# Attention and MLP in one kernel: the opening's loads, row copies, memsets and transposes in another order

## The chip, the cores and the metric

The kernel runs on one core of one Trainium2 chip. The metric is the device time of one execution in microseconds (us); the profile shows one such execution, taken by the hardware profiler. The engines are named as in the profile: PE is TensorE (matrix products, PEld its weight loads), DVE is VectorE, ACT is ScalarE, POOL is GpSimd, SP is SyncE, which here only issues transfers. SBUF is the memory on the core from which the engines work, PSUM the banks into which TensorE writes. "L311" is line 311 of the kernel.

## What is computed

Eight batches of causal attention with eight heads of 64 columns over 576 positions, with a decay that is a running sum of log f, and after it a two-layer MLP with a nonlinearity:

```python
scale = 1.0 / np.sqrt(D)
scores = scale * np.matmul(q, k.transpose(0, 1, 3, 2))
cum = np.cumsum(np.log(np.clip(f, 0.0001, 1.0)), axis=-1)
decay = cum[:, :, :, None] - cum[:, :, None, :]
scores = np.where(causal, -1000000000.0, scores + decay)
attn = np.exp(scores - np.max(scores, axis=-1, keepdims=True))
attn = attn / (np.sum(attn, axis=-1, keepdims=True) + 1e-09)
x = np.matmul(attn, v)            # then heads side by side: 4608 x 512
h = x @ w_in                      # w_in 512 x 2048
out = (h - np.tanh(h)) @ w_out    # w_out 2048 x 512
```

## The kernel before

**Pairs and tiles.** The work goes by pairs of heads: four pairs a batch, 32 in all. A pair has seven score tiles, numbered ti 0 to 6; tiles 0 to 2 belong to its first head, 4 to 6 to its second, tile 3 (`LAST`) holds the small last blocks of both. A score tile is some matrix products into a PSUM bank (L352; in batch 0 the causal mask is added by a further product with `late`, L355), an exp on ScalarE (L361, output `e`, or `el` for tile 3) and, from batch 1 on, a masking select on GpSimd (L371). `values` (L389) multiplies the exps with v; `divide` (L398 to L400) scales the result on VectorE into `xn`; `turn` brings xn into `XR`, the MLP's input, in batch 0 by a TensorE transpose and a copy (L417 to L421).

**Transposed q and k.** `trans` turns a pair's q or k on TensorE (six small products, L298) into a PSUM bank and copies it in two halves to QT or KT; the string handed over says by which engine and when: "V" VectorE (L311), "A" ScalarE (L309); a pair of letters listed in the line `now = ...` (before: "VA" and "Vv") has its second half put off until `rest` is called. With "AV" both halves are issued at once. Before pair 0, `split` gives four copies of 288 columns in place of two of 576.

**Decay rows.** QT and KT have 67 rows: 64 of the head, and three that bring the decay into the product. They are made from the running sum `cum` (scan, L187) as two fp16 parts, `chi` (L189) and `clo` (L190). For head 0 of batch 0 the rows are written by engines: QT's by ScalarE (L572), KT's by the VectorE copy of L191. The other heads' rows are transfers from chi and clo, made by `bulk` for batch 0 (two on SP's queue, one on GpSimd's, L211 to L213) and by `load_aug` for the later batches.

**Loads.** Nearly all loads are issued by GpSimd, in program order with its other work: q and k by pairs of heads (`load_qk`, L102), v by a whole head (`load_v_head`, L127), by a block of positions (`load_v_block`, L131), and the last 64 positions of all heads (`load_v_rest`, L123); w_in in two parts (L222), w_out in two (L226). Those of the body stand in the table `LOADS`, keyed by (pair, tile).

**Order.** It is written out by hand: `start` (L570) has the transposes of pair 0, its first two score tiles, and filler products on `warm` (`unread`, L566, results unused); then `bulk`, and then for each pair the list that `att_items` makes, tile by tile, with MLP pieces between its items from pair 4 on. `mlp1` (L451, tanh at L456, sum at L462) works a 128-column tile of w_in at a time, `mlp2_plain` (L492) and `mlp2` (L517) the second layer. Each engine takes its instructions in program order and waits where one's inputs or banks aren't ready. The exps have ten buffers, score tiles two banks (a third in batch 0), the early transposes three.

**Memsets.** Batch 0's padding is cleared by VectorE near the top; batch 1's (KT's padding columns, the unused rows of v's last block, v's column of ones, the third `el` buffer) by GpSimd in `last`, issued in pair 1.

Of the kernel before, what the change touches and what calls it, by code (L numbers as in the profile page):

```python
# [9 lines left out]
FP16 = mybir.dt.float16  # L10
# [4 lines left out]
PITCH = 640  # L15
VW = 66
# [5 lines left out]
def kernel(  # L22
# [10 lines left out]
    nc = tc.nc  # L33
# [96 lines left out]
    def load_v_block(b, n, h0, h1):  # L130
# [13 lines left out]
    nc.scalar.activation(out=expo, in_=warm[0:1, 0:1], func=AF.Ln)  # L144
    id16 = cst.tile([P, P], FP16)
    nc.vector.memset(id16, 0.0)
    nc.gpsimd.affine_select(out=id16, in_=id16, compare_op=ALU.not_equal,
                            fill=1.0, base=0, pattern=[[-1, P]], channel_multiplier=1)
    load_qk(qn, q, 0, 0, 2)
# [12 lines left out]
    per = cst.tile([NX, 6], FP32)  # L162
    nc.vector.memset(vn[0][D:P, NJ - 1, :, :], 0.0)
    mul_k, add_k, mul_l, mul_q, add_q, both = (per[:, i:i + 1] for i in range(6))
    EL = [cst.tile([P, 192], FP16, tag=f"el{i}", name=f"el{i}") for i in range(3)]
    load_v_rest(0)
    load_v_head(0, 0)
    load_v_head(0, 1)
    nc.gpsimd.affine_select(out=late, in_=late, compare_op=ALU.is_ge, fill=-60000.0,
                            base=0, pattern=[[1, P]], channel_multiplier=-1)  # L170

    r_hi, r_one = (id16[0:NX, NH + g:NH + g + 1] for g in (0, 2))
    nc.vector.tensor_scalar(out=both, in0=r_one, scalar1=-inv_qscale, scalar2=inv_qscale, op0=ALU.mult, op1=ALU.add)
# [5 lines left out]
    for e in EL[0:2]:  # L179
        nc.vector.memset(e, 0.0)  # L180
    nc.vector.tensor_scalar(out=lf, in0=lf, scalar1=0.0001, scalar2=1.0,
                            op0=ALU.max, op1=ALU.min)
    nc.vector.memset(vn[0][:, :, :, D:VW], 1.0)
    nc.scalar.activation(out=lf, in_=lf, func=AF.Ln)
    nc.scalar.activation(out=expo, in_=lf[0:1, 0:1], func=AF.Exp)
    cum = TQ[0][0:NX, :, :].rearrange("p c s -> p (c s)").bitcast(FP32)[:, S:2 * S]
# [1 line left out]
                                 op0=ALU.mult, op1=ALU.add)  # L188
    nc.vector.tensor_scalar(out=chi, in0=cum, scalar1=mul_k, scalar2=add_k, op0=ALU.mult, op1=ALU.add)  # L189
    nc.vector.scalar_tensor_tensor(out=clo, in0=cum, scalar=mul_l, in1=chi, op0=ALU.mult, op1=ALU.subtract)  # L190
    nc.vector.tensor_copy(out=KT[0][NH:NX, 0, 0:S], in_=clo[NH:NX, :])  # L191

    def aug_rows(b):
        i, h0 = b % 2, 0 if b else 1
# [12 lines left out]
    const_rows(0)  # L207

    def bulk():
        (k_hi, chi_0), (k_lo, clo_0), (q_hi, _) = aug_rows(0)  # L210
        nc.sync.dma_start(out=k_hi, in_=chi_0)  # L211
        nc.gpsimd.dma_start(out=q_hi, in_=chi_0)
        nc.sync.dma_start(out=k_lo, in_=clo_0)  # L213
        load_qk(qn, q, 0, 4, 6)
        load_qk(kn, k, 0, 4, 6)
        load_qk(qn, q, 0, 6, H)
        load_qk(kn, k, 0, 6, H)
        for n in range(NJ - 1):
            load_v_block(0, n, 2, H)
# [5 lines left out]
    def load_wout(e0, e1):  # L225
        nc.gpsimd.dma_start(out=wout[:, :, e0:e1], in_=moe_w_out[:, e0:e1].rearrange("(t p) e -> p t e", p=P))  # L226

    LOADS = {(0, 1): [lambda: load_qk(qn, q, 1, 0, 2), lambda: load_qk(kn, k, 1, 0, 2)],
             (0, 4): [lambda: load_qk(qn, q, 1, 2, 4), lambda: load_qk(kn, k, 1, 2, 4)],
             (1, 0): [lambda: load_win(0, DFF // 2)],  # L230
             (1, 2): [lambda: load_qk(qn, q, 1, 4, H)],
             (1, 5): [lambda: load_qk(kn, k, 1, 4, H)],
             (2, 1): [lambda: load_v_rest(1), lambda: load_v_head(1, 0)],
             (2, 4): [lambda: load_v_head(1, 1), lambda: load_win(DFF // 2, DFF)],
             (4, 0): [lambda: load_wout(0, HE)],
             (5, 1): [lambda: load_wout(HE, DM)]}
    for n in range(NJ - 1):
# [49 lines left out]
    def trans(b, c, src, dst, early, copies, split=False):  # L287
        pn, g3 = S // NT6, NT6 // 2
        if early:
            t32 = m_bank("t32")  # L290
        elif KEPT and src is kn:
            t32 = ps_m.tile([P, UW], FP32, tag=f"m{KEPT[0]}", name="t32")
        else:
            t32 = ps_tr.tile([P, UW], FP32, tag="tr", name="t32")
        t16 = t32.bitcast(FP16)[:, 0:2 * S // 2].rearrange("p (a g n) -> p a g n", a=2, g=g3)
        for a in range(2):
            for g in range(g3):
                nc.tensor.transpose(out=t16[:, a, g, :],  # L298
                                    in_=src[b % 2][:, 2 * c + a, 2 * g:2 * g + 2, :],
                                    identity=id16[0:pn, 0:pn])  # L300
        parts = [(a, e) for a in range(2) for e in range(2)] if split else [(slice(0, 2), e) for e in range(2)]

        def copy(a, e, eng):
            if split:
                a = slice(a, a + 1)
            to = dst[b % 2][0:D, 2 * c:2 * c + 2, e:S:2].rearrange("d a (p g) -> d a p g", g=g3)[:, a]
            of = t16[e * D:(e + 1) * D, :, :, :].rearrange("d a g p -> d a p g")[:, a]
            if eng == "A":
                nc.scalar.activation(out=to, in_=of, func=AF.Copy)  # L309
            else:  # L310
                nc.vector.tensor_copy(out=to, in_=of)  # L311

        todo = [lambda a=a, e=e, eng=eng: copy(a, e, eng) for (a, e), eng in zip(parts, copies)]
        now = 1 if copies in ("VA", "Vv") else 2
        for fn in todo[:now]:
            fn()
        if now == 1:
            LATER.extend(todo[now:])
        return todo[now:]
# [250 lines left out]
    def start():  # L570
        unread(47)
        nc.scalar.activation(out=QT[0][NH:NX, 0, :], in_=cum[NH:NX, :], func=AF.Identity, bias=add_q[NH:NX, :], scale=mul_q[NH:NX, :])  # L572
        q_rest = trans(*pairs[0], qn, QT, True, "AAAA", True)
        for fn in q_rest:
            fn()
        unread(6)
        k_rest = trans(*pairs[0], kn, KT, True, "VVVV", True)
        unread(34)
        scores(*pairs[0], 0)
        for fn in k_rest:  # L580
            fn()
        scores(*pairs[0], 1)
        unread(2)

    def last():
        nc.gpsimd.memset(KT[1][:, :, S:PITCH], 0.0)
        nc.gpsimd.memset(vn[1][D:P, NJ - 1, :, :], 0.0)
        nc.gpsimd.memset(vn[1][:, :, :, D:VW], 1.0)
        nc.gpsimd.memset(EL[2], 0.0)

    def att_items(p):
        def put(fn, *args):
# [7 lines left out]
        for ti in range(len(TILES)):  # L600
# [4 lines left out]
                items.append((lambda: load_aug(1), False))  # L605
            if p == 0 and ti in (2, 5, 6):
                put(unread, {2: 6, 5: 4, 6: 2}[ti])
            if p == 1 and ti == 3:
                put(last)
            for load in LOADS.get((p, ti), ()):  # L610
                items.append((load, False))
            at_q, at_k = (1, 2) if p == 0 else (None, 0) if early else (0, 2) if p == NPAIR else (0, 3)
            if ti == 5 and p < NPAIR - 1:
                put(trans, *pairs[p + 2], qn, QT, True, "VV")
            if p in (2 * NPAIR - 1, 2 * NPAIR, 2 * NPAIR + 1) and (ti % 2 or ti == 0):
                items.append((rest, False))
# [7 lines left out]
                    put(mlp1, 0, ti - 4, 1)  # L624
                    items.append((rest, False))
            if ti == at_k and p < 2 * NPAIR - 1 and p != NPAIR:
                put(trans, *after, kn, KT, early, "AV" if p in (0, 2) else "VV")
            if p == NPAIR:
                if ti == 0:
                    put(turn, *pairs[1])  # L630
                elif ti == 1:
                    put(turn, *pairs[p - 2])
                    put(values, *before)
                    put(mlp1, 0, 0, 0)
                elif ti == 2:
                    put(mlp1, 0, 1, 0)
                    put(turn, *before, True)
                    put(trans, *after, kn, KT, early, "Vv")
            elif early and ti in (2, 4) and before:
                put(values, *before, (ti // 2 - 1,))  # L640
            elif not early and ti == 2 and before:
                put(values, *before, (0, 1), p == NPAIR + 2)
            if p < NPAIR:
# [70 lines left out]
```

## Time and profile before

| | us |
|---|---|
| median of 3 runs | 338.89 (338.81 to 339.19) |
| profiled execution | 338.77 |
| its span, first to last instruction | 337.1 |
| first scores of pair 0 (L352) | 9.12 |
| first exp (L361) | 9.60 |
| first product of mlp1 (L451) | 27.28 |
| first part of w_in landed | 26.2 |
| second part of w_in landed | 35.3 |

The landings are an issue's start plus the time to landing that the profile gives for it (16.05 + 10.1 and 21.89 + 13.4). The landings of the other loads that matter here, in the same way: q and k of heads 0, 1 at 5.05 and 5.8; of heads 2, 3 at 7.65 and 8.4; the rest of v at 8.8, value heads 0 and 1 at 9.4 and 10.3; the chi rows of QT at 10.9; q and k of heads 4, 5 at 11.1 and 12.0; of heads 6, 7 at 14.2 and 14.7; the four value blocks at 15.6, 16.4, 17.0 and 17.6.

How to read it: a timeline row gives the start, the duration, the engine, the line, the operation with its output and inputs and shapes, how many follow each other, and in brackets the time that the engine stood idle before it and what ended this. Pieces of the chain of waits follow each other in time; each was released by the one before it. PE counts as busy also with filler products.

### The profile page before, as it was taken

The page shows a single profiled execution, that of the slowest core. Times are in us where ns is not written, and L with a number is a line of the kernel's source. Part 1 is how long each engine was busy: PE and PEld are TensorE (multiplying, and loading weights), DVE is VectorE, ACT ScalarE, POOL GpSimd, SP SyncE. Part 2 cuts the span into 40 slices and gives each one's busy share as a digit, 9 for nine tenths or more (in the row PEclk, how much of TensorE's full clock was granted, in tenths as well). Part 3 has the DMA queues.
Part 4 walks back from the last instruction along what each step waited for, and adds up shares of the span by engine and source line. Part 5 has one row for each costly group of instructions (what it writes and reads, how often), then busy time and mean ns, then how long its engine had stood idle before and what let it go on. Part 6 is the DMA issues. An engine that isn't in the chain of part 4 may idle for free.

```text
span 337.1 us, 8726 instructions
## 1 busy us (share of the span) xinstructions
PE 330.0 (98%) x3313; PEld 235.6 (70%) x3313; DVE 260.8 (77%) x509; ACT 233.2 (69%) x438; POOL 163.2 (48%) x321
## 2 busy tenths in 40 slices
PE   8899999999999999999999999999999999999996
PEld 8775558875687558845888888656865686486485
DVE  7998986659887886778867896788668866966865
ACT  6997777978977886788677867787558733632630
POOL 8977467775667564767377637722322210000000
PEclk9999999999999999999999999999999999999999
DMA  9999999999979997999899999990130022002003
GB/s 113 143 203 202 186 198 165 184 159 172 142 87 190 136 134 72 164 152 139 94 122 187 118 112 117 163 132 18 51 113 2 19 65 97 2 31 95 0 12 116
DMA packets 147468, 38.82 MB, mean 115 GB/s; under 512 B 128181, under 2 KB 146335, under 8 KB 147426
## 3 DMA queue, kind: packets, MB, share of 16 engines
q0 software_dynamic: 94528, 18.37, 75.5%
q1 hardware_dynamic: 52892, 19.89, 32.4%
q8 instruction: 26, 0.43, 0.6%
q14 instruction: 16, 0.13, 0.2%
q10 hardware_dynamic: 6, 0.01, 0.0%
HBM read 36.85 MB, written 9.44 MB: 137 GB/s over the span
## 4 chain that ended last, share of the span: by engine, by line
PE 90%; DVE 7%; ACT 2%; issue 1%; ACTq 0%
PE hps L451 36%; PE ops L517 29%; PE ps L352 11%; PE av L389 8%; PE ops L492 4%; DVE KT L311 2%; DVE QT L311 1%; PE t L298 1%; ACT e L361 1%; DVE xn L400 1%; DVE gq L462 0%; DVE TQ L187 0%; ACT th L456 0%; PE x L417 0%; DVE clo L190 0%
## 5 line engine op out<-in xcount | busy, mean ns | idle before, releaser
L451 PE MATMUL hps<-XR,win 128*128 128x512 f16 (+1 forms) x640 | 140.7, 357 | 0.3 <-DVE gq L462 0.3
L456 ACT ACTIVATE th<-hps 128x512 f32<-128x512 f32 x144 | 86.6, 602 | 55.5 <-PE hps L451 53.5
L361 ACT ACTIVATE e<-ps 128x512 f16<-128x512 f32 x192 | 110.2, 597 | 8.9 <-PE ps L352 7.4
L462 DVE TENSOR_TENSOR gq<-hps,th 128x512 f16<-128x512 f32 x144 | 98.0, 687 | 23.6 <-ACT th L456 22.0
L371 POOL TENSOR_SCALAR_AFFINE_SELECT e<-e 128x128 f16<-128x128 f16 x168 | 60.7, 364 | 71.5 <-ACT e L361 68.7
L451 PEld LDWEIGHTS <-win 128*128 128x128 f16 x640 | 57.7, 97 | 49.0 <-issue 1.1
L352 PE MATMUL ps<-QT,KT 67*128 67x64 f16 (+4 forms) x384 | 76.5, 276 | 2.0 <-DVE KT L311 1.4
L517 PEld LDWEIGHTS <-gq 128*128 128x128 f16 x640 | 60.3, 97 | 11.1
L517 PE MATMUL ops<-wout,gq 128*128 128x256 f16 x512 | 63.2, 272 | 0.0
L352 PEld LDWEIGHTS <-KT 67*128 67x128 f16 x384 | 36.4, 98 | 23.4 <-DVE KT L311 2.0
L389 PEld LDWEIGHTS <-e 128*128 128x128 f16 x896 | 32.3, 97 | 3.6
L389 PE MATMUL av<-vn,e 128*128 128x65 f16 x896 | 33.6, 193 | 0.0
L517 PE MATMUL ops<-W,sq 128*128 128x256 f16 x256 | 31.2, 272 | 0.0
L131 POOL DMA_DIRECT2D vn<-in_v_dram x32 | 28.0, 877 | 6.5 <-DMA win<-in_moe_w_in_dram 2.9
L400 DVE TENSOR_TENSOR xn<-av,rs 128x640 f16<-128x640 f32 x32 | 26.4, 825 | 1.3 <-DVE rs L399 0.2
L517 PEld LDWEIGHTS <-sq 128*128 128x128 f16 x256 | 24.1, 97 | 3.4
L108 POOL DMA_DIRECT2D kn<-in_k_dram x25 | 21.2, 848 | 2.1 <-issue 1.8
L108 POOL DMA_DIRECT2D qn<-in_q_dram x25 | 21.2, 848 | 1.8 <-issue 1.4
L371 POOL TENSOR_SCALAR_AFFINE_SELECT el<-el 128x128 f16<-128x128 f16 x28 | 9.3, 333 | 26.1 <-ACT el L361 25.8
L398 DVE TENSOR_SCALAR rs<-av 128x10 f32<-128x10 f32 x32 | 5.2, 163 | 18.2 <-PE av L389 17.0
L532 ACT ACTIVATE m<-ops 128x512 f32<-128x512 f32 x16 | 9.5, 596 | 10.9 <-PE ops L517 10.9
L484 DVE TENSOR_TENSOR gq<-gq 128x512 f16<-128x512 f16 x32 | 17.1, 533 | 0.0
(83 smaller groups left out, 311.8 us busy)
## 6 DMA issues: line engine op xcount, KB each, us to landing
out_dram<-ost SPq DMA_DIRECT2D x34, 256.0 KB
vn<-in_v_dram POOLq DMA_DIRECT2D x24, 128.0 KB, 6.2
qn<-in_q_dram POOLq DMA_DIRECT2D x20, 128.0 KB, 5.0
kn<-in_k_dram POOLq DMA_DIRECT2D x20, 128.0 KB, 5.6
win<-in_moe_w_in_dram POOLq DMA_DIRECT2D x2, 1024.0 KB, 11.8
wout<-in_moe_w_out_dram POOLq DMA_DIRECT2D x2, 1024.0 KB, 15.6
XR<-xn SPq DMA_TRANSPOSE x56
qn<-in_q_dram POOLq DMA_DIRECT2D x6, 144.0 KB, 4.6
```

The costliest lines, as they stand in the source:

```text
L108: nc.gpsimd.dma_start(out=dst[b % 2][0:pn, n, :].rearrange("p (h d) -> p h d", h=H), in_=src[b, :, n * P:n * P + pn, :].rearrange("h p d - ...
L131: nc.gpsimd.dma_start(out=vn[b % 2][:, n, h0:h1, 0:D], in_=v[b, h0:h1, n * P:(n + 1) * P, :].rearrange("h p d -> p h d"))
L352: nc.tensor.matmul(out=ps[:, col:col + n], lhsT=kt[0:rows, h, j * P:(j + 1) * P], rhs=qt[0:rows, h, i0:i0 + n], start=True, stop=cut == 0)
L361: nc.scalar.activation(out=e[:, lo:hi], in_=ps[:, lo:hi], func=AF.Exp, bias=-SHIFT, scale=qscale)
L371: nc.gpsimd.affine_select(out=view, in_=view, compare_op=ALU.is_ge, fill=0.0, base=0, pattern=pat, channel_multiplier=-1)
L389: nc.tensor.matmul(out=av[:, a, ib, :], lhsT=E.pop((b, c, a, j, ib)), rhs=vn[b % 2][:, j, 2 * c + a, 0:D + 1], start=(j == 0), stop=(j == ib))
L400: nc.vector.tensor_tensor(out=xn.rearrange("p i (a d) -> p a i d", a=2), in0=av[:, :, :, 0:D], in1=rs.to_broadcast([P, 2, NJ, D]), op=ALU. ...
L451: nc.tensor.matmul(out=hps[:, o:o + n], lhsT=win[:, ci, ft * P:(ft + 1) * P], rhs=XR[:, ci, t:t + n], start=(ci == 0), stop=(ci == NCH - 1))
L456: nc.scalar.activation(out=th, in_=hps, func=AF.Tanh, scale=-1.0)
L462: nc.vector.tensor_tensor(out=GQ[(u, i)][:, half, kt, :], in0=hps, in1=th, op=ALU.add)
L484: nc.vector.tensor_tensor(out=LHS[name](u, i)[:, ks], in0=LHS[x](u, i)[:, ks], in1=LHS[y](u, i)[:, ks], op=op)
L517: nc.tensor.matmul(out=ps[:, m, :], lhsT=LHS[lhs](u, kt // 4)[:, kt % 4, m * P:(m + 1) * P], rhs=rhs[:, kt, :], start=(fresh and (apart or ...
```

## The change

In words, in program order:

- The third `el` buffer's memset and KT[1]'s padding move up: the padding to GpSimd's front, ahead of the select that makes the identity; the `el` memset behind the select that makes `late`.
- Q's heads 4, 5 of batch 0 are loaded right behind the first four loads; value head 0 then goes ahead of the rest of v; value head 1 moves into `bulk`, behind k's heads 4, 5.
- The two memsets of vn[1] move to VectorE, behind the clip of f.
- The transfer of the chi rows to QT moves out of `bulk`, ahead of the copy of clo's rows into KT, and that copy is made by GpSimd instead of VectorE.
- w_in is split 7:9 tiles instead of 8:8; its first part is issued in (0, 4), where k's heads 2, 3 of batch 1 stood, and these move to (1, 0).
- Pair 1's k copies go by "Av" (ScalarE's half at once, VectorE's put off) instead of "AV". Pair 2's q is transposed at tile 3 of pair 0 (by "Vv", with `rest` right behind) instead of tile 5. Pairs 3 and 4 have q transposed at tile 6 instead of 5.
- Pair 1's first values come at tile 3 of pair 2 instead of tile 2.
- Three filler products fewer (31 for 34) ahead of the first scores.

```diff
+    EL = [cst.tile([P, 192], FP16, tag=f"el{i}", name=f"el{i}") for i in range(3)]
+    nc.gpsimd.memset(KT[1][:, :, S:PITCH], 0.0)
     nc.gpsimd.affine_select(out=id16, in_=id16, compare_op=ALU.not_equal,
...
-    EL = [cst.tile([P, 192], FP16, tag=f"el{i}", name=f"el{i}") for i in range(3)]
+    load_qk(qn, q, 0, 4, 6)
+    load_v_head(0, 0)
     load_v_rest(0)
-    load_v_head(0, 0)
-    load_v_head(0, 1)
     nc.gpsimd.affine_select(out=late, in_=late, compare_op=ALU.is_ge, fill=-60000.0,
                             base=0, pattern=[[1, P]], channel_multiplier=-1)
+    nc.gpsimd.memset(EL[2], 0.0)
...
-    nc.vector.memset(vn[0][:, :, :, D:VW], 1.0)
+    nc.vector.memset(vn[1][D:P, NJ - 1, :, :], 0.0)
+    for t in vn:
+        nc.vector.memset(t[:, :, :, D:VW], 1.0)
...
-    nc.vector.tensor_copy(out=KT[0][NH:NX, 0, 0:S], in_=clo[NH:NX, :])
+    nc.gpsimd.dma_start(out=QT[0][D + 2:D + 3, 1:H, :], in_=chi[1:H, :])
+    nc.gpsimd.tensor_copy(out=KT[0][NH:NX, 0, 0:S], in_=clo[NH:NX, :])
...
     def bulk():
-        (k_hi, chi_0), (k_lo, clo_0), (q_hi, _) = aug_rows(0)
+        (k_hi, chi_0), (k_lo, clo_0), _ = aug_rows(0)
         nc.sync.dma_start(out=k_hi, in_=chi_0)
-        nc.gpsimd.dma_start(out=q_hi, in_=chi_0)
         nc.sync.dma_start(out=k_lo, in_=clo_0)
-        load_qk(qn, q, 0, 4, 6)
         load_qk(kn, k, 0, 4, 6)
+        load_v_head(0, 1)
         load_qk(qn, q, 0, 6, H)
...
+    WF = 7 * P
...
-             (0, 4): [lambda: load_qk(qn, q, 1, 2, 4), lambda: load_qk(kn, k, 1, 2, 4)],
-             (1, 0): [lambda: load_win(0, DFF // 2)],
+             (0, 4): [lambda: load_qk(qn, q, 1, 2, 4), lambda: load_win(0, WF)],
+             (1, 0): [lambda: load_qk(kn, k, 1, 2, 4)],
...
-             (2, 4): [lambda: load_v_head(1, 1), lambda: load_win(DFF // 2, DFF)],
+             (2, 4): [lambda: load_v_head(1, 1), lambda: load_win(WF, DFF)],
...
-        now = 1 if copies in ("VA", "Vv") else 2
+        now = 1 if copies in ("VA", "Vv", "Av") else 2
...
-        unread(34)
+        unread(31)
...
-    def last():
-        nc.gpsimd.memset(KT[1][:, :, S:PITCH], 0.0)
-        nc.gpsimd.memset(vn[1][D:P, NJ - 1, :, :], 0.0)
-        nc.gpsimd.memset(vn[1][:, :, :, D:VW], 1.0)
-        nc.gpsimd.memset(EL[2], 0.0)
...
-            if p == 1 and ti == 3:
-                put(last)
...
-            if ti == 5 and p < NPAIR - 1:
+            if ti == 6 and 0 < p < NPAIR - 1:
                 put(trans, *pairs[p + 2], qn, QT, True, "VV")
...
-                put(trans, *after, kn, KT, early, "AV" if p in (0, 2) else "VV")
+                put(trans, *after, kn, KT, early, "Av" if p == 0 else "AV" if p == 2 else "VV")
+            if p == 0 and ti == 3:
+                put(trans, *pairs[2], qn, QT, True, "Vv")
+                items.append((rest, False))
...
-            elif early and ti in (2, 4) and before:
-                put(values, *before, (ti // 2 - 1,))
+            elif early and ti in (3 if p == 2 else 2, 4) and before:
+                put(values, *before, (ti // 4,))
```

## The prediction

> **What bounds the kernel now.** I read the page first, then the chain of waits of the first 45 us, then the timelines of ScalarE, VectorE, GpSimd and TensorE up to 40 us, then the landing of each load. The page says where a saving can count at all:
>
> ```profile
> PE 330.0 (98%) x3313; PEld 235.6 (70%) x3313; DVE 260.8 (77%) x509; ACT 233.2 (69%) x438; POOL 163.2 (48%) x321
> ```
>
> TensorE is busy for 330.0 of 337.1 us, and its work in the body isn't touched. Between 36 and 60 us it is busy 23.77 of 24. So the change can only move the time at which this full stretch begins; whatever it saves in the opening arrives at the end once, undiluted. What sets that time is in the chain of waits of the opening (start, duration, piece):
>
> ```profile
> 6.91 0.83 DVE clo L190
> 7.74 0.02 issue
> 7.76 0.30 DVE KT L191
> 8.06 0.03 issue
> 8.09 0.47 DVE KT L311
> 8.57 0.01 issue
> 8.58 0.49 DVE KT L311
> 9.07 0.05 issue
> 9.12 0.39 PE ps L352
> ...
> 11.38 0.81 ACT KT L309
> 12.19 0.02 issue
> 12.22 0.81 DVE KT L311
> ...
> 25.21 0.84 DVE xn L400
> 26.05 0.04 issue
> 26.09 0.45 PE x L417 x5
> ```
>
> The reader is to see VectorE in nearly every piece: clo, the 0.30 us copy of its rows into KT, the two copies for head 0, the first scores at 9.12; after a detour over ScalarE, VectorE again from 12.22 to 26.05, where TensorE takes over. But ScalarE is nearly as full (its timeline; in brackets the idle time before a row):
>
> ```profile
> 9.60 1.78 ACT L361 ACTIVATE e<-ps 128x512 f16<-128x512 f32 x3 [0.29 <-PE ps L355]
> 11.38 0.81 ACT L309 ACTIVATE KT<-t 64x576 f16<-64x576 f16 x1
> 12.06 0.24 ACT L361 ACTIVATE el<-ps 128x128 f16<-128x128 f32 x1
> 12.20 3.39 ACT L361 ACTIVATE e<-ps 128x512 f16<-128x512 f32 x6
> ...
> 16.50 1.68 ACT L361 ACTIVATE e<-ps 128x512 f16<-128x512 f32 x3 [0.19 <-PE ps L352]
> ```
>
> From 9.60 to 16.3 it never rests. And ScalarE reaches VectorE through TensorE's order: pair 1's second group of values can only follow a score tile that waits for a PSUM bank which an exp frees:
>
> ```profile
> 19.36 0.38 PE L352 MATMUL ps<-QT,KT 67*128 67x512 f16 x1 [0.30 <-ACT e L361]
> ```
>
> Those values end at 20.25, and VectorE's division of pair 1 begins at 20.28. So at 20.28 two chains meet with 0.03 us between them, and from there to 26.05 VectorE has no gap. A gain on one chain alone is lost there.
>
> **The change, part by part.**
>
> *Rows of clo copied by GpSimd.* VectorE loses its 0.30 us copy, so KT's copies begin at 7.76, not 8.09: 0.33 earlier, with head 0's two done at 7.76 + 0.49 + 0.49 = 8.74. The first scores also need GpSimd's copy, which stands behind GpSimd's whole queue. That queue, by before's rows: the new KT memset at the front (67x512 took 0.60 at 17.49) can begin between 0.51, the end of the last GpSimd row, and about 0.9, where VectorE's first row stands; so the identity's select moves from 1.22 to between 1.22 and 1.5. I take +0.25, since nothing on the other queues begins before 0.81. The loads then begin at 1.80, 2.57, 3.20, 3.82 for heads 0 to 3, q's heads 4, 5 at 4.54 (0.68), value head 0 at 5.22 (0.77), the value rest at 5.99 (0.71), the select for late at 6.70 (0.55), EL[2]'s memset at 7.25 (0.26), the chi transfer at 7.50 (0.54), the copy at 8.04.
>
> GpSimd's copy of 3x576 has no row. Floor 0.30 (VectorE's own), ceiling 1.64 (576/128 selects of 0.364). The nearest row is the memset, 0.60 for 512 a partition, hence 0.68 for 576: done at 8.72, level with VectorE's 8.74. The first scores start at 8.79 instead of 9.12. The Trainium skill (GPSIMD Engine Reference, Engine selection) speaks against this move: elementwise work belongs on VectorE, GpSimd being some 2x slower with two inputs and roughly line-rate with one. Its best loop of 1.8 cycles an element at 1.2 GHz (the same page, Performance versus the Vector engine) gives an estimate of 0.86 us, the copy done at 8.90, and the scores 0.18 later than in my sum.
>
> ScalarE's first exp follows the first scores by 0.48 (9.60 against 9.12), so it could start at 9.27; but its own four QT copies run until 9.31. ScalarE gains **0.29**. TensorE's three dropped fillers (0.06 each) cost and give nothing: it waited 0.92 before the first scores.
>
> *The chi transfer* is issued at 7.50 instead of 7.17. It landed 3.7 later, q's 144 KB loads in 3.4 at best, so it lands between 10.9 and 11.2. Scores tile 3 (first use of head 1's q row) ran at 11.18 and is now wanted at 10.89. So the wait is 0 to 0.31 us; behind it on TensorE stand the tile-3 scores, the moved transposes of pair 2 (0.26) and scores tile 4, for which ScalarE waits. That costs ScalarE between nothing and 0.23. I take 0.09: **net gain 0.20**.
>
> *Pair 2's q transposes moved up, with the order "Av" and "Vv".* Before, VectorE idles 0.34 until 12.22 for ScalarE's half of pair 1's k. Now its next instruction is the first half of pair 2's q, whose load is issued at 4.54 rather than 7.70. So VectorE is ahead by 0.33 + 0.34 = 0.67 to 0.70 at about 14 us. The k half itself ends at about 13.2 instead of 13.02, still under the 13.50 at which the next scores run. This lead doesn't last: division 0 needs values whose TensorE rows ran without a gap from 13.50 to 16.12 and shift with ScalarE; at 20.28 TensorE's values decide, and they shift by ScalarE's 0.20. The 0.5 left over becomes VectorE idle time ahead of divisions 0 and 1.
>
> *Batch 1's memsets.* On VectorE 0.28 + 0.12 us fall into its 0.66 us wait for the logarithm (4.25 to 4.91), 0.26 to spare; without that cover they would cost up to 0.40 straight on the chain. GpSimd loses 1.57 us at 17.49, while it is ahead of need: nothing.
>
> *Bulk loads.* Behind the copy, GpSimd issues k's heads 4, 5 at 8.72 instead of 8.37, value head 1 at 9.36 (needed at 15.5: landing by 14.5 at the 5.1 us of its neighbours, free), and the four value blocks from 11.4 instead of 10.24. The last block landed at 17.6 and was used from 18.32. By the 1.15 of delay it lands at about 18.8; pair 1's first values, put one tile later, first touch it at about 18.4. The 0.3 us bank wait at 19.06 covers that difference: nothing, with 0 to 0.3 as bounds.
>
> *w_in 7:9.* The first part landed at 26.2 and was read from 27.28. It is an eighth smaller and one k load (0.8 to 1.8 us) earlier, against up to 1.4 of lateness on the queue: 24 to 26, free. K's heads 2, 3 of batch 1 land by 27 and are transposed at 29.2: free. Tile 7 of w_in now comes with the second part, which landed at 35.3, and is read at 37.58: free by about 2 us, or 0.9 if the queue is 1.4 late.
>
> *Later transposes* (ti 6 for 5): VectorE's order is the same; pair 4's q is transposed by about 20.7, wanted at 21.2. Free.
>
> **Sum.** 0.33 at the first scores, cut to 0.29 by ScalarE's copies, cut to 0.20 by chi, and 0.20 at 26.09. The profiled execution took 338.77 (span 337.1 and 1.67 around it), so 338.57; it lies 0.12 under the median of the runs, 338.89, from which the same step gives 338.69. I take **338.6**.
>
> **Rivals.**
>
> *VectorE's lead goes through (0.20).* If ScalarE and the banks aren't what holds 20.28, and 0.7 us arrive whole: 338.07 to 338.19. For it: the chain of waits is VectorE's from 12.22 on. Against it: the 0.30 us bank wait, and ScalarE without idle time.
>
> *GpSimd's copy is late (0.12).* Past about 1.0 us (8.04 + 1.0 = 9.04 against 9.07 before) the first scores lose instead of gaining; at the ceiling of 1.64 ScalarE starts at 10.19, not 9.60. Time 338.9 to 339.5. It would also be the case in which the skill's page is right to keep the copy off GpSimd.
>
> *The second part of w_in is late (0.10), slower.* Tile 7 is read at 37.4, in the stretch where TensorE has no gap, so each us past 37.4 is a whole us of time. It decides from a landing 2.1 us later than 35.3. For it: the loads' queue is full (landings of 10 to 13 us after 16 us), GpSimd issues some 1.2 us later at 11.4, and 128 more columns stand in this part. Against: the same bytes are ahead of it, and the dropped memsets let GpSimd catch up by 19 us. A landing at 38.2 to 38.6 gives 339.6 to 340.0.
>
> **Numbers.** Forecast 0.58, within 338.4 to 338.8. A measurement of this kernel can tell about 0.2% from no change, 0.68 us: 338.21 to 339.57. Faster by more: the first rival, 0.20. Slower by more: the last and a part of the copy's tail, 0.15. The rest 0.65. The range runs from 338.0 (0.7 from 338.77, and a little more) to 339.4 (the copy's ceiling), leaving out the late w_in and a little beyond the lead.
>
> **What would show it.** The first scores at about 8.8 and the first exp at 9.31; a GpSimd copy of about 0.68 ending near 8.7; VectorE without the wait at 11.9, but with new waits of 0.2 to 0.5 for values ahead of divisions 0 and 1; TensorE's x transposes at about 25.9. I am wrong if those waits don't appear and the x transposes stand at 25.4, if the first scores are later than 9.1, or if TensorE waits on w_in near 37.

## The result, and the profile after

The changed kernel takes 339.41 us (median of 22 runs, 338.84 to 341.43), the kernel before 338.85 beside it (22 runs, 338.74 to 339.58). The ratio is 1.002, with a 95% interval of 1.001 to 1.0029: slower, by 0.56 us in the medians. Its best run is as fast as the kernel before; what has changed is how often a run loses something. The profiled execution took 339.77 (span 338.1), 1.0 us more than the profiled one of before, so the trace below shows one of the dearer runs (seventh of 22). (Ratios follow the mean of the runs compared and leave disturbed ones out, so they are not exactly the quotients of the medians.)

The page, sections 1 and 4 (busy time; what the chain that ended last consists of):

```profile
PE 330.3 (98%) x3310; PEld 235.7 (70%) x3310; DVE 262.1 (78%) x510; ACT 232.9 (69%) x438; POOL 165.0 (49%) x320
PE 80%; DVE 10%; DMA 4%; SPq 2%; ACT 2%; issue 1%; ACTq 0%; DVEq 0%
```

TensorE has the same work as before, in a longer span. What is new is in the second line: 4% DMA and 2% SP's queue. Before, this line was "PE 90%; DVE 7%; ACT 2%; issue 1%": no transfer was in the chain.

**The opening gained nothing.** The chain of waits of the first 45 us, after (start, duration, piece):

```profile
6.30 0.95 DVE chi L193
7.28 0.81 DVE clo L194
8.09 0.38 DVE KT L316
8.49 0.49 DVE KT L316
...
9.12 0.38 PE ps L357
...
26.09 0.45 PE x L422 x5
```

The 0.30 us copy is gone from between clo and KT. Yet KT begins at 8.09 as before, the first scores at 9.12 as before, x at 26.09 as before. Chi takes 0.95 where it took 0.59: the 0.36 eat the 0.33. The timelines of VectorE and GpSimd, after, show what lies beside chi (in brackets idle time and what ended it):

```profile
6.30 0.94 DVE L193 TENSOR_SCALAR chi<-TQ,per 67x576 f16<-67x576 f32 x1
```

```profile
6.37 0.34 POOL L170 TENSOR_SCALAR_AFFINE_SELECT late<-late 128x128 f16<-128x128 f16 x1
6.62 0.30 POOL L172 MEMSET el<- 128x192 f16 x1
7.53 0.54 POOL L195 DMA_DIRECT2D QT<-chi  x1 [0.61 <-DVE chi L193]
8.25 0.66 POOL L196 COPY KT<-clo 3x576 f16<-3x576 f16 x1 [0.18 <-DVE clo L194]
```

and the same two instructions before:

```profile
6.30 0.58 DVE L189 TENSOR_SCALAR chi<-TQ,per 67x576 f16<-67x576 f32 x1
```

```profile
6.48 0.55 POOL L169 TENSOR_SCALAR_AFFINE_SELECT late<-late 128x128 f16<-128x128 f16 x1
```

Before, the select started 0.18 behind chi and took 0.55; after, it starts 0.07 behind chi and takes 0.34, and now chi takes longer. One of the two pays 0.26 to 0.36 (the select alone takes 0.29, as d below shows). Two things differ: the select starts 0.11 us earlier against chi, since the loads ahead of it were put in another order, and a memset of `el` now follows it while chi runs. Which of the two turns the price over to chi isn't shown, since no run has the one without the other. The Trainium skill (GPSIMD Engine Reference, Specifications) says that GpSimd's SBUF interfaces are shared with VectorE, with contention where VectorE's instruction is in a two-port mode or has two SBUF inputs. The rows show a price where the two engines overlap; whether the shared interfaces are the reason, and which mode chi runs in, no row shows.

**The loads are later, and stay later.** GpSimd now waits 0.61 for chi and 0.18 for clo, and its copy takes 0.66, all ahead of the bulk of the loads. The first value block's issue, before and after (the second row holds all four blocks):

```profile
10.24 0.85 POOL L131 DMA_DIRECT2D vn<-in_v_dram  x1
```

```profile
11.55 3.35 POOL L131 DMA_DIRECT2D vn<-in_v_dram  x4
```

Landings (issue plus time to landing, us):

| load | before | after |
|---|---|---|
| k heads 4, 5 of batch 0 | 12.0 | 12.6 |
| first value block | 15.6 | 16.5 |
| w_in, first part | 26.1 | 26.6 |
| w_in, second part | 35.3 | 37.2 |
| w_out, first part | 43.5 | 46.0 |
| w_out, second part | 55.2 | 58.7 |
| rest of v, batch 2 | 60.9 | 65.0 |
| k of batch 3, last | 72.0 | 77.4 |
| rest of v, batch 3 | 82.8 | 87.2 |

The profile's DMA rates for 8 to 10, 10 to 12 and 12 to 14 us are 83, 123 and 114 GB/s after, 114, 144 and 149 before. The lateness isn't made good but grows from 0.9 to about 5 us. Late issue is only its beginning: batch 2's value blocks are issued at 44.62 in both traces and its rest of v at 50.54 and 50.53, yet they land 2 and 4 us later. So by then the lateness no longer lies in the issue.

**Where TensorE loses it.** The values' start times are equal in both traces up to 71.8 us; then after is 0.23 later (81.23 for 81.00), and from 107 us on 1.0 later (108.26 for 107.25), to the end. The chain of waits between 60 and 112 us, after:

```profile
65.69 7.37 DMA XR<-xn
...
86.83 7.06 DMA TK<-kn
...
93.91 0.45 DVE KT L120
...
105.10 0.69 DVE ost L541
...
105.84 1.03 PE ops L522 x8
```

XR's transposes release TensorE at 73.11 (the 0.23), and k's transposes for batch 3 release VectorE at 93.91; from batch 3 on these are transfers on SP's queue (L113). SP's queue, before and after:

```profile
68.94 6.83 SPq L113 DMA_TRANSPOSE TQ<-qn  x5
...
79.11 6.45 SPq L113 DMA_TRANSPOSE TK<-kn  x5
```

```profile
69.01 8.30 SPq L113 DMA_TRANSPOSE TQ<-qn  x5
...
80.75 7.30 SPq L113 DMA_TRANSPOSE TK<-kn  x5
```

The same five transposes take 8.30 for 6.83 us and 7.30 for 6.45, and end 2.5 us later in all. Most of this lies in single transposes (2.21 us at 75.10, 2.05 at 83.37; before, the longest of the ten took 1.59). None of them waits for its own load: q of batch 3 has landed by 69.7, its last block's turn is at 75.10; k has landed at 77.4, and its transposes begin at 80.75. What differs is that loads which used to be done are still landing beside them. That this slows them is argued from the comparison only: between 69 and 77 us the queues moved less after, 137 GB/s for 158. VectorE's copy before, then VectorE and TensorE after:

```profile
91.83 0.44 DVE L120 COPY KT<-TK 64x1152 f16<-64x1152 f16 x1
```

```profile
93.91 0.45 DVE L120 COPY KT<-TK 64x1152 f16<-64x1152 f16 x1 [1.77 <-DMA TK<-kn]
```

```profile
105.84 1.03 PE L522 MATMUL ops<-wout,gq 128*128 128x256 f16 x8 [0.72 <-DVE ost L541]
```

Before, the copy had no wait. After, VectorE stands 1.77 us, makes up for part of it, and is 0.72 us late with `ost` at 105.8. 0.23 and 0.72 are 0.95 of the 1.0 us.

### The profile page after: what moved, and what is told of

Read it like the earlier page. It is cut to its first block, busy times and chain, and to the rows that moved or that the text cites. A ratio compares the mean times of both kernels' runs of the same rounds, so it can differ in the third digit from the quotient of the medians.

```text
span 338.1 us, 8721 instructions
## 1 busy us (share of the span) xinstructions
PE 330.3 (98%) x3310; PEld 235.7 (70%) x3310; DVE 262.1 (78%) x510; ACT 232.9 (69%) x438; POOL 165.0 (49%) x320
## 3 DMA queue, kind: packets, MB, share of 16 engines
q0 software_dynamic: 94528, 18.37, 77.2%
## 4 chain that ended last, share of the span: by engine, by line
PE 80%; DVE 10%; DMA 4%; SPq 2%; ACT 2%; issue 1%; ACTq 0%; DVEq 0%
PE hps L456 32%; PE ops L522 26%; PE ps L357 10%; PE av L394 7%; PE ops L497 2%; DMA XR<-xn 2%; DMA TK<-kn 2%; SPq L113 2%; DVE KT L316 1%; PE t L303 1%; DVE QT L316 1%; ACT e L366 1%; DVE sq L489 1%; DVE gq L467 1%; DVE xn L405 1%
## 5 line engine op out<-in xcount | busy, mean ns | idle before, releaser
L376 POOL TENSOR_SCALAR_AFFINE_SELECT e<-e 128x128 f16<-128x128 f16 x168 | 62.3, 375 | 66.6 <-ACT e L366 64.4
L403 DVE TENSOR_SCALAR rs<-av 128x10 f32<-128x10 f32 x32 | 5.2, 162 | 17.6 <-PE av L394 16.5
```

The costliest lines, as they stand in the source:

```text
L376: nc.gpsimd.affine_select(out=view, in_=view, compare_op=ALU.is_ge, fill=0.0, base=0, pattern=pat, channel_multiplier=-1)
```

## The experiments

Three theories. The **queue** theory (Q): GpSimd's new waits and copy hold the loads back, and the lateness costs TensorE wherever a reader has no margin, far behind the opening. The **collision** theory (P): chi against the select takes the opening's gain. The **w_in** theory (L): the split and move of w_in cost. R in the expectations is the rival that something else costs, such as the transposes in another order. Each kernel below ran 8 to 12 times; "before" beside them had medians of 338.81 to 338.85. The last three columns are of the profiled execution alone; "x" is the start of the x transposes that stand at 26.09 in both kernels.

| run | median (range) | ratio (95%) | x | second w_in part | k of batch 3, last |
|---|---|---|---|---|---|
| a_copy_back | 339.50 (339.24 to 344.41) | 1.0019 (1.0011 to 1.0028) | 26.56 | 36.9 | 74.2 |
| b_copy_only | 339.08 (338.58 to 340.14) | 1.0006 (0.9997 to 1.0014) | 25.84 | 36.0 | 73.6 |
| c_win_only | 338.89 (338.77 to 341.38) | 1.0006 (0.9993 to 1.0019) | 26.11 | 35.3 | 72.3 |
| d_late_behind | 339.86 (338.82 to 345.12) | 1.0028 (1.0013 to 1.0043) | 26.26 | 36.9 | 75.6 |
| e_loads_first | 338.97 (338.61 to 339.45) | 1.0003 (0.9995 to 1.0012) | 26.38 | 35.6 | 72.2 |
| f_hold_early | 339.82 (339.24 to 341.32) | 1.0032 (1.002 to 1.0044) | 26.36 | 37.2 | 75.1 |
| g_hold_later | 339.68 (338.89 to 342.72) | 1.0033 (1.0017 to 1.005) | 26.34 | 37.5 | 77.2 |
| h_changed_loads_first | 339.46 (338.67 to 343.69) | 1.0038 (1.0012 to 1.0064) | 26.37 | 35.4 | 72.4 |
| i_extra_load | 339.03 (338.76 to 341.11) | 1.0016 (1.0002 to 1.0029) | 26.11 | 35.6 | 77.8 |
| j_no_k2 | 338.76 (338.73 to 339.28) | 0.9999 (0.999 to 1.0007) | 26.51 | 36.7 | 71.4 |
| k_copy_memsets | 338.71 (338.60 to 339.87) | 1.0003 (0.9995 to 1.0012) | 26.11 | 36.3 | 77.6 |
| p_win_back | 339.18 (338.49 to 342.55) | 1.0015 (0.9997 to 1.0032) | 29.94 | 35.6 | 74.9 |

**a: the changed kernel with the copy back on VectorE and the chi transfer back in `bulk`.**

```diff
-    nc.gpsimd.dma_start(out=QT[0][D + 2:D + 3, 1:H, :], in_=chi[1:H, :])
-    nc.gpsimd.tensor_copy(out=KT[0][NH:NX, 0, 0:S], in_=clo[NH:NX, :])
+    nc.vector.tensor_copy(out=KT[0][NH:NX, 0, 0:S], in_=clo[NH:NX, :])
...
         nc.sync.dma_start(out=k_hi, in_=chi_0)
+        nc.gpsimd.dma_start(out=q_hi, in_=chi_0)
```

> The changed kernel with one part undone: VectorE copies clo's rows into KT again, and the chi transfer stands in bulk again, so that GpSimd never waits for clo. Theory Q (queue): in the changed kernel GpSimd idles 0.61 us for chi and 0.18 for clo and copies for 0.66 before it issues k's heads 4, 5 at 8.85; the loads of the next 90 us are all later for it (by 1.3 at 11.55, 1.9 when the second part of w_in lands, 4 to 5 at 65 to 77), TK's transposes land 2 us late near 94, and TensorE loses 0.7 to 1.0. By Q the loads come about 0.8 to 1.0 earlier than in the changed kernel, w_in's second part lands near 36, and the time is 338.8 to 339.1. Rival L (order of the loads): the larger second part of w_in and k's heads 2, 3 behind its first part make the lateness; then the time stays at 339.3 to 339.6.

The time stays at 339.5. Chi is still 0.93 us, and with the copy on VectorE again the first exp stands at 9.96 and x at 26.56, 0.47 later than before; the value blocks are issued at 10.75, 0.8 earlier than in the changed kernel but 0.5 later than before. The range that the queue theory gave (338.8 to 339.1) was missed. Taking the copy back uncovers the collision at full price, and in this profiled run (339.33) the loss is the opening's, so the run doesn't test the queue.

**b: the kernel before with only the copy on GpSimd and the chi transfer ahead of it.**

```diff
-    nc.vector.tensor_copy(out=KT[0][NH:NX, 0, 0:S], in_=clo[NH:NX, :])
+    nc.gpsimd.dma_start(out=QT[0][D + 2:D + 3, 1:H, :], in_=chi[1:H, :])
+    nc.gpsimd.tensor_copy(out=KT[0][NH:NX, 0, 0:S], in_=clo[NH:NX, :])
...
-        nc.gpsimd.dma_start(out=q_hi, in_=chi_0)
```

> The kernel before with one part alone: the chi transfer ahead of a copy of clo's rows by GpSimd. Q: GpSimd issues q's heads 4, 5 and all behind it 0.7 to 1.0 later than before, and the time is 339.1 to 339.5, with runs spread wider than before's. L: the copy costs nothing, 338.8, or gains up to 0.3 if the first exp comes at 9.31.

ScalarE's timeline in b:

```profile
9.34 1.08 ACT L361 ACTIVATE e<-ps 128x512 f16<-128x512 f32 x2
```

No wait in brackets: ScalarE goes straight from its own copies to the first exp, 0.26 earlier than before, and x stands at 25.84, 0.25 earlier. Chi takes 0.57 here. So the gain that the prediction computed for this step exists, and the profiled run has it (338.58, 0.19 under before's). The median doesn't: 339.08. The loads are 0.8 late at 11 us (value blocks issued at 11.03 for 10.24), and 1.6 at k of batch 3.

**c: the kernel before with only w_in's split and place changed.**

```diff
-             (0, 4): [lambda: load_qk(qn, q, 1, 2, 4), lambda: load_qk(kn, k, 1, 2, 4)],
-             (1, 0): [lambda: load_win(0, DFF // 2)],
+             (0, 4): [lambda: load_qk(qn, q, 1, 2, 4), lambda: load_win(0, 7 * P)],
+             (1, 0): [lambda: load_qk(kn, k, 1, 2, 4)],
...
-             (2, 4): [lambda: load_v_head(1, 1), lambda: load_win(DFF // 2, DFF)],
+             (2, 4): [lambda: load_v_head(1, 1), lambda: load_win(7 * P, DFF)],
```

> The kernel before with one part alone: w_in split 7:9, its first part ahead of k's heads 2, 3. Q: no load is issued later by more than the waits between them, 338.8 to 338.95. L: 339.2 to 339.5.

No change can be measured; nine of eleven runs lie within 338.77 to 338.95. The other two, 339.37 and 341.38, widen the interval, whose upper end is 0.64 us. In the medians the split costs 0.08, so by itself it doesn't make the 0.56.

**d: the changed kernel with the select for `late` and the `el` memset behind the copy.**

```diff
-    nc.gpsimd.affine_select(out=late, in_=late, compare_op=ALU.is_ge, fill=-60000.0,
-                            base=0, pattern=[[1, P]], channel_multiplier=-1)
-    nc.gpsimd.memset(EL[2], 0.0)
...
     nc.gpsimd.tensor_copy(out=KT[0][NH:NX, 0, 0:S], in_=clo[NH:NX, :])
+    nc.gpsimd.affine_select(out=late, in_=late, compare_op=ALU.is_ge, fill=-60000.0,
+                            base=0, pattern=[[1, P]], channel_multiplier=-1)
+    nc.gpsimd.memset(EL[2], 0.0)
```

> The changed kernel with the select that makes late and the third el buffer's memset moved on GpSimd's queue from ahead of the chi transfer to behind the copy. In the changed kernel chi took 0.94 us instead of 0.58 while that select and that memset ran. Theory P (VectorE and GpSimd block each other there): chi takes 0.58 again, the first scores come at 8.8 and the first exp at 9.31, and TensorE's x transposes of pair 2 stand 0.2 to 0.3 earlier than 26.09; the time falls by those 0.3 against the changed kernel as far as the late loads allow: 338.9 to 339.3. Rival: the 0.94 has another cause (the length of the row is chance, or the early memsets on VectorE); then chi stays near 0.94 and the first scores at 9.1.

Chi is 0.57, the select 0.29, the first scores at 8.76, the first exp at 9.34: with nothing of GpSimd beside it, chi has its old time, and the collision is shown. But the time is no better (339.86; 338.9 to 339.3 was expected). TensorE's timeline in d:

```profile
11.56 0.19 PE L357 MATMUL ps<-QT,KT 67*128 67x64 f16 x1 [0.42 <-DVE QT L316]
```

That is head 1's product in tile 3. The wait takes back the opening's gain (x at 26.26). It is put down to a VectorE copy; the chi rows had landed at 11.0, before it began, and what else it was for isn't shown. And the loads are later still: value blocks issued at 11.76, VectorE waiting 1.2 us for TK near 93.7, and TensorE 0.26 us for XR's transposes at 73.47.

**e: the kernel before with the copy on GpSimd, but behind q's heads 4, 5, and the chi transfer on SP's queue.**

```diff
                             base=0, pattern=[[1, P]], channel_multiplier=-1)
+    load_qk(qn, q, 0, 4, 6)
...
-    nc.vector.tensor_copy(out=KT[0][NH:NX, 0, 0:S], in_=clo[NH:NX, :])
+    nc.gpsimd.tensor_copy(out=KT[0][NH:NX, 0, 0:S], in_=clo[NH:NX, :])
...
         nc.sync.dma_start(out=k_lo, in_=clo_0)
-        load_qk(qn, q, 0, 4, 6)
+        nc.sync.dma_start(out=q_hi, in_=chi_0)
```

> The kernel before with the copy of clo's rows on GpSimd, but q's heads 4, 5 issued ahead of it, while GpSimd would wait for chi and clo anyway, and the chi transfer on SP's queue behind clo's. By Q the opening keeps its gain (first exp 9.34, pair 2's x transposes at 25.8 to 25.9, as in the kernel with the copy alone), the loads behind the copy come no later than before (k's heads 4, 5 at about 8.4), and the time is 338.5 to 338.7, spread like the kernel before. If the copy on GpSimd costs in another way than by the loads behind it: 339.0 to 339.2, as in the kernel with the copy alone. A third outcome: the chi rows land later by SP's queue and tile 3's scores wait; then the x transposes stand at 26.0 or later and the time is 338.8.

The loads are on time, chi takes 0.57, the first exp is at 9.34; but TensorE waits 0.8 us for the chi rows, third on SP's queue, and x is at 26.38. This is the dearest of the eleven runs (339.45): 0.29 of its loss is the opening's, and 0.27 is a wait of TensorE for XR's transposes at 215.3 us. So such a wait also occurs with these loads on time. The median, 338.97, can't be told from before's; what its opening looked like no trace shows.

**f and g: the kernel before with five further `el` memsets on GpSimd, 1.59 us in one piece, ahead of the bulk loads (f) or behind the value blocks (g).**

```diff
         nc.sync.dma_start(out=k_lo, in_=clo_0)
+        for n in range(5):
+            nc.gpsimd.memset(EL[2], 0.0)
         load_qk(qn, q, 0, 4, 6)
```

> The kernel before with one cost added: five memsets of the third el buffer (0.26 us each, 1.3 in all) on GpSimd in bulk, ahead of q's heads 4, 5; nothing else changes. Theory Q, now in a narrower form (hole): what costs is that the loads' stream runs dry near 8 to 12 us and all later loads land late for the next 90 us. By Q q's heads 4, 5 are issued at about 8.9 instead of 7.70, the value blocks at 11.5 instead of 10.24, w_in's second part lands 1 to 1.5 later than 35.3, the first exp stays at 9.60, and the time is 339.1 to 339.6 with single runs over 340. Rival R (something else in the changed kernel, as its transposes in another order): late loads cost nothing, 338.8 to 338.95.

> The kernel before with the same five memsets, but behind the four value blocks of batch 0, where the loads lag 4.6 to 5.4 us behind their issue against 3.4 at best, so that the stream has 1.2 to 2 us of work in store. By Q (hole) the store covers most of the 1.3 us: w_in's second part lands at 35.3 to 35.8, the time is 338.8 to 339.0. If lateness of issue by itself counts, it is the same as in the kernel with the early hold, 339.1 to 339.6. By R 338.8 to 338.95, as there.

Both cost 0.9 to 1.0 us. f's waits:

```profile
PE hps L453 <- DMA win<-in_moe_w_in_dram: 0.6, 1, 0.6
```

In both, the first w_in part lands at 28.3 and TensorE waits 0.6 to 0.7 us for it; x is 0.25 to 0.27 late as well. Holding GpSimd's loads back does cost time, and here at the first reader, which the changed kernel still reaches in time. A narrower idea, that a hold behind the value blocks would be covered by what is already loading, fell: g costs about the same as f. These two runs show a price for late loads, but not the changed kernel's own place.

**h: the changed kernel with k's heads 4, 5 and value head 1 ahead of the copy, the select behind it, and the chi transfer on SP's queue.**

```diff
...
+    load_qk(kn, k, 0, 4, 6)
+    load_v_head(0, 1)
     nc.gpsimd.tensor_copy(out=KT[0][NH:NX, 0, 0:S], in_=clo[NH:NX, :])
+    nc.gpsimd.affine_select(out=late, in_=late, compare_op=ALU.is_ge, fill=-60000.0,
+                            base=0, pattern=[[1, P]], channel_multiplier=-1)
+    nc.gpsimd.memset(EL[2], 0.0)
...
         nc.sync.dma_start(out=k_lo, in_=clo_0)
-        load_qk(kn, k, 0, 4, 6)
-        load_v_head(0, 1)
+        nc.sync.dma_start(out=q_hi, in_=chi_0)
```

> The changed kernel with GpSimd's queue reordered: k's heads 4, 5 and value head 1 ahead of the copy, the select for late and the el memset behind it, the chi transfer on SP's queue behind clo's. By Q and P together: chi 0.58, first exp 9.34, the value blocks issued at about 10.3 as in the kernel before, w_in's second part landing near 35.5, and 338.5 to 338.8. By R (transposes in another order cost) 339.2 to 339.5 in spite of all that.

The loads are on time (35.4, 72.4), and the profiled run is near before's (338.97). TensorE's waits in h:

```profile
PE ps L357 <- DMA QT<-chi: 0.5, 1, 0.5
```

x is at 26.37, and the time is not better: 339.46, where queue and collision theory together had forecast 338.5 to 338.8 and the rival 339.2 to 339.5. What its ordinary runs lose no trace shows. Three runs of 340.9 to 343.7 have a mean TensorE clock of 0.985 to 0.994; what that can be, p shows. The changed kernel's own long runs are of another kind: those of 341.2 and 341.4 have a clock of 1.0 and 0.998.

**i: the kernel before with one more load, unread: 14 times 128 rows of v behind w_out's first part.**

```diff
-             (4, 0): [lambda: load_wout(0, HE)],
+             (4, 0): [lambda: load_wout(0, HE), load_extra],
...
```

> The kernel before with one load more: fourteen heads' first 128 positions of v (1792 rows of 256 bytes) into a tile that nothing reads, behind w_out's first part in (4, 0). The opening and w_in are as before. Q (late loads cost in the body): all later loads land some 1.5 to 2 us later, q's and k's last blocks of batch 3 at 68 and 74 instead of 66.7 and 72.0, v's last of batch 3 at 84 to 85 instead of 82.8, TK's transposes end later than 92, VectorE waits for them as in the changed kernel, and the time is 339.1 to 339.6 with a wider spread. Rival R: no change, 338.8 to 338.95.

The opening is untouched. The loads behind it come 2 to 6 us late (k of batch 3 at 77.8, as late as in the changed kernel), SP's transposes take 8.03 and 6.91 us, and VectorE's waits have the changed kernel's line:

```profile
DVE KT L120 <- DMA TK<-kn: 0.9, 1, 0.9
```

In the profiled run TensorE lost nothing by it (span 337.1, as before); over twelve runs the time rises by 0.18 in the median and spreads to 341.1. So lateness in the stream alone gives the longer transposes, the wait, the spread and a mean loss that can't be told from the changed kernel's (ratio 1.0016 against 1.002).

**j: the changed kernel without batch 2's load of k (batch 2's scores use batch 0's keys).**

```diff
-            add((p0, 5), load_qk, kn, k, b, 0, H)
```

> The changed kernel without one load: batch 2's k (576 KB) is left out, so that batch 2 works on batch 0's keys. All loads behind it land some 2.5 to 3 us earlier than in the changed kernel, near or ahead of the kernel before. By Q the 0.23 us at 73 and the 0.78 us near 105 are gone and the time is 338.7 to 338.95, spread like the kernel before. By R (something in the order of the transposes, memsets or values) it stays at 339.3 to 339.5.

This speaks most clearly. Every other part of the change is in place, and the opening is the changed kernel's (chi 0.94), yet the time is 338.76, nine of eleven runs within 338.73 to 338.77. (The profiled run is one of the other two, 339.18: TensorE waits 0.4 us for clo's rows, x is at 26.51, and that 0.4 is all it loses.) The loads behind the missing one are back where before had them (71.4 for k of batch 3). SP's queue in j:

```profile
69.37 7.19 SPq L113 DMA_TRANSPOSE TQ<-qn  x5
...
79.84 6.48 SPq L113 DMA_TRANSPOSE TK<-kn  x5
```

The transposes take 7.19 and 6.48 us, not 8.30 and 7.30, and VectorE doesn't wait for TK. With room in the stream, the changed kernel's loss and its spread are gone. The kernel before without this load was not run. Over all the runs but p, whose whole body is late, the first five transposes take 6.83 to 7.46 us where k of batch 3 has landed by 74.2, and 7.56 to 8.61 where it lands at 75.1 or later.

**p: h with w_in as before (8:8, in its old place).**

```diff
...
-    WF = 7 * P
+    WF = 8 * P
...
-             (0, 4): [lambda: load_qk(qn, q, 1, 2, 4), lambda: load_win(0, WF)],
-             (1, 0): [lambda: load_qk(kn, k, 1, 2, 4)],
+             (0, 4): [lambda: load_qk(qn, q, 1, 2, 4), lambda: load_qk(kn, k, 1, 2, 4)],
+             (1, 0): [lambda: load_win(0, WF)],
```

> The changed kernel with GpSimd's loads ahead of the copy (as in the run before) and w_in's split and place put back to 8:8 behind k's heads 2, 3. That run spread from 338.67 to 343.69 though its profiled execution showed its loads on time and nothing lost in the body. If the split makes the spread: 338.9 to 339.1, no run over 340. If the spread has another source: 339.3 to 339.6 as there.

The profiled run is one of the long ones, 342.55. Tile 3's product waited 1.45 us for the chi rows and ran at 12.60, and the windows view gives the granted clock behind it (columns: busy us and instructions of each engine, clock, DMA share, GB/s):

```profile
12.00:16.00 4.00, 3.35 (x24) 2.43 (x25) 2.29 (x3) 1.91 (x4) 4.00 (x7) 0.58 1.97 153
16.00:20.00 4.00, 4.00 (x52) 3.25 (x51) 1.60 (x2) 2.50 (x6) 4.00 (x7) 0.57 1.24 162
```

From 12 to 20 us TensorE's granted clock was 0.58 and 0.57 (0.50 from 13 to 16), and x stands at 29.94, 3.85 us late: all of the 3.8 by which this run is longer than before's. So here a 1.45 us wait was followed by a slow clock; after the shorter waits of e (0.79) and h (0.53) the clock stayed at 1.00. The Trainium skill (TensorE: Matmul & The Clock Gate, Part 1: The HAM clock gate) puts the drop to half rate after an idle window of about 3.4 us; the gap here was less than half of that, and between 9 and 11 us TensorE was busy for 1.86 of 2, so in this run a shorter gap came before the drop. Three other runs of p, at 338.49 to 338.64, are among the fastest of the study. So the long runs stay with w_in's old split; this one came with the wait for chi's rows on SP's queue. For the other long runs of p and h that is argued from their clocks, not seen in a trace.

**k: b with batch 1's memsets off GpSimd.**

```diff
+    nc.gpsimd.memset(KT[1][:, :, S:PITCH], 0.0)
...
-    for e in EL[0:2]:
+    for e in EL:
...
+    nc.vector.memset(vn[1][D:P, NJ - 1, :, :], 0.0)
+    for t in vn:
+        nc.vector.memset(t[:, :, :, D:VW], 1.0)
...
-            if p == 1 and ti == 3:
-                put(last)
...
```

> The kernel before with two parts: the chi transfer ahead of GpSimd's copy, and batch 1's memsets moved off GpSimd's queue (KT's padding to its front, the rest to VectorE's wait for the logarithm). The first exp at 9.34, the x transposes at 25.85, as with the copy alone; the loads behind the copy 0.7 to 0.8 later than before, but from 17.5 us on 0.8 earlier at issue. If late issue near 20 us matters: 338.6 to 338.9. If only the early hole counts (the stream has lost 0.7 us near 9 and can't win it back): 339.0 to 339.1, as with the copy alone.

The best median of all, 338.71, and six of eleven runs at 338.60 to 338.71; but four others lie at 339.2 to 339.9, and it can't be told from before. The profiled run was a dear one (339.87): VectorE's memsets put chi 0.12 later, k of batch 3 landed at 77.6, TensorE is 0.24 late at 81.20 as in the changed kernel, and its timeline has the changed kernel's wait at the very same place:

```profile
105.84 1.03 PE L520 MATMUL ops<-wout,gq 128*128 128x256 f16 x8 [0.65 <-DVE ost L539]
```

No version beat the kernel before beyond doubt. Not tried: a chi transfer that stays on GpSimd's queue with all loads still on time.

## Why the prediction was wrong

Forecast was 338.6 with a gain of 0.20; the result is 339.41, a loss of 0.56, and 0.01 above the range's end.

- **The failed step that decided: "bulk loads", put at "nothing, with 0 to 0.3 as bounds".** The issue times were right (value blocks forecast from 11.4, seen at 11.55), and the near readers waited neither for values nor for w_in, though by a narrower margin than forecast: the first w_in part landed at 26.6 (forecast 24 to 26, read at 27.28), the second at 37.2 (limit in the forecast: 37.4). What failed was to compare a late load only with its next reader. In the traced run what paid stood 60 to 95 us further on and didn't read the late loads: transposes on SP's queue, longer while late loads were landing (8.30 for 6.83 us), then VectorE (1.77), then TensorE (0.72 there, and 0.23 for XR at 73). j, which gives the stream room, takes the loss away; i, which delays the stream alone, brings back VectorE's wait and the spread. The rival "slower" had the right cause, late loads, at the wrong place: w_in.
- **The failed step in the opening: KT's copies "at 7.76, not 8.09".** The 0.33 was there, but chi grew by 0.36. The forecast moved the select by 0.22 later on GpSimd (6.70 for 6.48); it came 0.11 earlier (6.37), mostly since the new memset in front cost the loads only 0.05 and not 0.25, and the forecast never asked what GpSimd's select and memset would meet on VectorE. b and e, where the select starts 0.17 behind chi and no memset follows, and d and h, where neither is beside it, have chi at 0.57; a and j, with the changed order, at 0.93 and 0.94.
- **Right: GpSimd's copy.** 0.68 forecast from the memset's row, 0.66 measured in every run that has it. The estimate of 0.86 from the Trainium skill (GPSIMD Engine Reference, Performance versus the Vector engine) was too high for this size. That VectorE makes this copy faster holds (0.30 here).
- **Right, in b: ScalarE limits the gain.** 0.35 at the first scores, 0.26 at the first exp, 0.25 at x; forecast 0.29 and 0.20 (with the chi transfer).
- **Half right: the lead of VectorE comes back as waiting.** A wait of 0.30 for values stands ahead of division 0 at 16.26, none ahead of division 1, and x didn't come earlier. Since chi took the 0.33, only the other half of the forecast lead was there to come back.
- **Not borne out: the 0.09 for chi's rows.** In the changed kernel they landed at 10.4, ahead of tile 3's first product at 11.16; the 0.18 between this tile's products stands in the trace of before as well. The waits that other runs have there are partly for other rows (0.43 for clo's in j; in d what it was for isn't shown). Where chi's transfer is third on SP's queue they are 0.5 to 1.4, far above the bound of 0.31.
- **Right: memsets under the logarithm, the later transposes, w_in's new order.** c shows the last by itself; for the others, no wait in the trace and j's time speak against a cost.

What stays open: f and g lose at w_in, so they don't price the later loss by itself. Why the lateness grows from 0.9 to 5 us isn't separated into loads that wait for their buffers and loads that slow each other. Whether the transposes are slowed by the loads' packets or by waits within SP's queue isn't shown, and e has a wait for XR with its loads on time. h, with the loads on time, was as slow in the median as the changed kernel, and its trace doesn't show why, so late loads needn't be the only thing that the changed order costs. The traces with the loss are of two dear runs (the changed kernel's and k's); what a run of the median, or one of 341 us, loses where, no trace shows.

## What to carry to other kernels

Where a kernel's loads form one stream without pauses, a delay at its head needn't be over at the next reader: follow it through the kernel, look also at transfers on other queues that run beside the late loads, such as transposes, and find the first place with little margin. A wait put on an engine that also issues the loads is a wait for all of them. Before instructions on GpSimd shift by a tenth of a microsecond, look at what VectorE does in that moment, and measure a step by itself before adding it to others: b had the gain, and the whole change didn't.

## What the runs showed of the hardware

- Chi (67x576, fp32 to fp16) on VectorE took 0.57 or 0.58 us when GpSimd's select started 0.17 or 0.18 behind it or not beside it, and 0.93 or 0.94 when the select started 0.07 behind it and a memset followed; the select took 0.54 or 0.55 and 0.34, and 0.29 where it stood behind GpSimd's copy (d, h, p).
- GpSimd's copy of 3x576 fp16 took 0.66 us in all runs that have it, VectorE's 0.30 (0.38 in f, with memsets on GpSimd beside it).
- A transfer of chi's rows was waited for by 0.5, 0.8 and 1.4 us when third on SP's queue, and by 0.2 at most when GpSimd issued it and the wait was put down to it (g).
- After a wait of 1.45 us near the start, TensorE's granted clock was 0.58 from 12 to 20 us (p); after waits of 0.79 and 0.53 it stayed at 1.00 (e, h).
- Five transposes on SP's queue took 6.83 us in the kernel before and 8.30, 8.03 and 8.61 where loads landed 5 to 6 us later (the changed kernel, i, k).
- Executions spread from 338.73 to 339.28 with room in the stream of loads (j) and from 338.84 to 341.43 without (the changed kernel).
